# One ring of 18 buffers for the raw and split q and k tiles of a fused attention and MLP kernel

## The chip, the cores and the metric

The kernel runs on one core of a Trainium2 chip. The metric is the device time of one execution in microseconds (us); less is better. In the profile PE is the matrix engine (PEld its weight loads), DVE the vector engine, ACT the scalar engine, POOL the GpSimd engine, and SP the engine that does nothing here but issue transfers (SPq is its queue).

## The reference

For 4 batches, 8 heads, 576 positions and a head size of 64, attention with a learned position bias is computed; its output is read as 2304 tokens of 512 values and goes through two MLP layers with 2048 hidden units. Cut to what matters:

```python
scores = scale * np.matmul(q, k.transpose(0, 1, 3, 2))
psi_rel, psi_i = np.log1p(np.abs(rel)), np.log1p(np.maximum(pos[:, None], 1.0))
bias = np.maximum((psi_rel / psi_i)[..., None] @ w1 + b1, 0.0) @ w2
scores = scores + bias.transpose(2, 0, 1)[None]
attn = np.exp(scores - np.max(scores, axis=-1, keepdims=True))
x = np.matmul(attn / (np.sum(attn, axis=-1, keepdims=True) + 1e-09), v)
h = x @ w_in;   x = (h * np.cos(h)) @ w_out
h = x @ w_in2;  out = (np.maximum(h, 0.0) + alpha * np.minimum(h, 0.0)) @ w_out2
```

## The kernel before

The program has five stages: attention, then the hidden layer and the output layer of the first MLP (h_phase0, o_phase), then the same of the second. The change touches attention alone, so the rest is told only as far as attention runs into it.

Attention works on 16 pairs: a pair n is two heads hp of one batch b. Pair n brings a q tile and a k tile of 128 partitions by 640 values. Their matrix products are made from split operands: `load_qk` lets q and k land as raw tiles rq and rk (SP issues both transfers), and `split_qk` lets POOL make a rounded part (qh, kh, line 421, a cast) and the rest (ql, kl, line 426, a subtraction). `emit_S` makes a score tile S from three products (qh kh, qh kl, ql kh). Pair 0 alone is used unsplit (`NFP` is 1): its raw tiles feed the products.

Each pair has five score tiles: S1 and S2 belong to unit A, S0, S3 and S4 to unit B. The first four pairs run all their units A first and their units B later, so that four pairs' q and k are alive at once; from pair 4 on a pair runs A, then B. There is one PSUM buffer for S, so the next S waits until both halves of the one before have been read by DVE (`emit_max`, line 459: scores plus bias, and the row maximum nm, for the bias tiles bt of the two heads). ACT then makes the exponential P (line 472). Transposes of P (T), the product with v (x) and the normalisation (R, N) fill PE between score tiles.

The bias is made beside this, at the start of the program: 36 groups g in the order 0 to 15, 32 to 35, 16 to 31. For a group DVE makes the hidden units u (line 132, a few by ACT, line 130), PE makes the sums bps (line 137), ACT makes the rows be (line 151) and SP writes them to a DRAM table bias_d (line 156). There are six buffers for be. A bias tile bt is read back from the table by SP (lines 385 to 393) when the groups that it needs have landed: bt0_1 and bt0_5 need groups 0 to 7, bt0_2 and bt0_6 groups 8 to 15.

Towards the end of attention a background list stages the MLP's weights, one step at a time, through tiles with one or two buffers: raw weights land (raw, line 181), ACT, DVE and POOL convert them (wc, wp, lines 211 to 221), DVE combines them (wt, line 264), ACT and POOL split them (sw, lines 237 and 239) and SP writes the parts to DRAM (line 254). The tile for sw has one buffer, so a split begins when the transfer of the one before has landed.

The program's order on each engine is not that of the code. A scheduler sorts all instructions by priority and by its own planned times, and it hands a tile a free buffer of its pool at that moment, not in turn. An engine then runs its instructions strictly in that order; SP too, so a transfer that waits for its buffer holds back every transfer behind it.

q and k have two pools. The first has one buffer for rq and one for rk, so raw q of pair n+1 can only land when ql of pair n is made, and raw k when kl is made. The second has four buffers each for qh, ql, kh and kl; pair 0's raw tiles take one of the four of qh and of kh. That makes 18 buffers of 2560 bytes per partition.

Of the kernel before, what the change touches and what calls it, by code (L numbers as in the profile page):

```python
# [9 lines left out]
F32 = mybir.dt.float32  # L10
F32R = mybir.dt.float32r
# [24 lines left out]
QC = S + 64  # L36
# [4 lines left out]
FIRST, SIDE, SMOD, BFIRST, BRATE, SPL, WS0, WSR, PER = 4, 6, 2, 8, 2.5, 3, 28, 3.2, 1.0  # L41
# [1 line left out]
START = ((0, 1), (1, 1), (0, 2), (1, 2), (2, 1), (2, 2), (3, 1), (3, 2))  # L43
KEEP = (1, 1)
ELAG = 1
NFP = 1
NDIR = 6
XA, HX = 2, 300
RING, LO = 4, 3
# [19 lines left out]
def attn_mlp_kernel(ctx: ExitStack, tc: tile.TileContext, a: dict, out: bass.AP):  # L69
# [256 lines left out]
    def attention():  # L326
        with ExitStack() as c:
# [9 lines left out]
            pos = {(n, s): j for j, (n, u, s) in enumerate(stages)}  # L337

            bt_p = c.enter_context(tc.tile_pool(name="bt", bufs=BTB))
            rq_p = c.enter_context(tc.tile_pool(name="rq", bufs=1))  # L340
            qk_p = c.enter_context(tc.tile_pool(name="qk", bufs=FIRST))
            v_p = c.enter_context(tc.tile_pool(name="vp", bufs=FIRST + 1))
            m_p = c.enter_context(tc.tile_pool(name="mp", bufs=6))
            P_p = c.enter_context(tc.tile_pool(name="PP", bufs=PBUF))
# [6 lines left out]
            qk = {}  # L351
# [43 lines left out]

            def load_qk(n):
                hp, b = pairs[n]
                p, x = (rq_p, "r") if n >= NFP else (qk_p, "h")
                rq, rk = (p.tile([128, QC], F32, tag=(t + x) if n < NFP else (x + t), name=f"r{t}{n}") for t in "qk")
                sy.dma_start(out=rq, in_=a["q"][b, hp])  # L400
                sy.dma_start(out=rk, in_=a["k"][b, hp])
                raws[n] = (rq, rk)
# [7 lines left out]
            def load_qkv(n):  # L410
                load_qk(n)
                load_v(n)

            def split_qk(n):
                if n < NFP:
                    qk[n] = raws.pop(n)
                    return
                t = []
                for r, nm in zip(raws.pop(n), "qk"):
                    hi, lo = (qk_p.tile([128, QC], F32R, tag=nm + x, name=f"{nm}{x}{n}") for x in "hl")  # L420
                    ge.tensor_copy(out=hi, in_=r)
                    t.append((r, hi, lo))
                yield
                qk[n] = [x for r, hi, lo in t for x in (hi, lo)]
                for r, hi, lo in t:
                    ge.tensor_tensor(out=lo, in0=r, in1=hi.bitcast(F32), op=ALU.subtract)
                    yield

            def emit_S(n, s):
                q, k = qk[n][::len(qk[n]) // 2]  # L430
                terms = ((q, k),)
                if n >= NFP:
                    qh, ql, kh, kl = qk[n]
# [161 lines left out]
            for n in range(2):  # L595
                load_qk(n)
                for _ in split_qk(n):
                    pass
            sy.dma_start(out=alpha, in_=a["alpha"])

            def rest():
                for n in range(2, FIRST):
                    load_qk(n)
                    yield
                    load_v(n - 2)
                    yield from split_qk(n)
                    done.add(n)
                for n in range(FIRST - 2, FIRST):
                    load_v(n)
                    yield  # L610
# [38 lines left out]
            while i < NS or pend_exp or waiting or fill:  # L649
                new = []  # L650
                if i < NS:
                    n, u, s = stages[i]
                    hp, b = pairs[n]
                    more_bias(max(BFIRST + int(BRATE * j), GNEED[s]))
                    for m in range(FIRST, NP):
                        f = pos[m, 1]
                        if i == f - 6:
                            load_qkv(m)
                            splits[m] = split_qk(m)
                        if f - SPL <= i < f:  # L660
                            next(splits[m], None)
                    while n not in done:
                        next(side, None)
                    pss = emit_S(n, s)
                    new = [(n, s, h) + emit_max(n, s, h, ps) for h, ps in enumerate(pss)]
# [334 lines left out]
    def h_phase1():  # L1000
        runs = [[(0, 512), (512, 1024)], [(1024, 1536), (1536, 2048)], [(2048, 2304)]]
        with ExitStack() as c:
# [78 lines left out]
            step(1000)  # L1081

    attention()
    pinned.append(1)
    h_phase0()
# [71 lines left out]
```

## Time and profile before

| what | value |
|---|---|
| median of three runs | 1146.52 us (1136.35 to 1147.46) |
| the profiled execution | 1133.93 us, span 1131.8 us from first to last instruction |
| busy PE, DVE, ACT, POOL | 1082.6, 820.8, 641.8, 247.6 us |
| attention, by PE's order | about 0 to 362 us, with the first products of h_phase0 from 347 us |

The span is 2.1 us shorter than the profiled execution's time. PE is busy for 96% of the span, so what can be gained is mostly in the 49 us in which PE is idle, and in the stretches in which its clock was granted at half. Times in the rows below count from the start of the span.

### The profile page before, as it was taken

To read this page: it belongs to the slowest core of one execution; us is meant where nothing else is said; L and a number is where in the kernel's file an instruction comes from. 1 tells how busy PE (TensorE), PEld (TensorE's weight loads), DVE (VectorE), ACT (ScalarE), POOL (GpSimd) and SP (SyncE) were. 2 spreads that over 40 slices of the span, in tenths; PEclk is the share of its full clock that TensorE was granted. 3 is DMA by queue.
4 is the path that set the end of the run, shared out by engine and by line. 5 is a ranking of instruction groups with operands and counts; after the bars stand their busy time and mean duration, and the time that the engine had idled before them with its cause. 6 is when DMAs were issued, how large, how long until landed. Compare 5 with 4: busy or idle time off the path is not lost.

```text
span 1131.8 us, 18836 instructions
## 1 busy us (share of the span) xinstructions
PE 1082.6 (96%) x7054; PEld 895.4 (79%) x7054; DVE 820.8 (73%) x1336; ACT 641.8 (57%) x1072; POOL 247.6 (22%) x248
## 2 busy tenths in 40 slices
PE   7698999999998998999999999899999999999998
PEld 2245666667666877888799999888888888999998
DVE  8886677777775799787876767767766756776673
ACT  6886667777775555555454444655655534444442
POOL 4304656656433121000000000112323210000000
PEclk9889999999999999999999999999999999999999
DMA  8656645666447774533766344555666549664621
GB/s 276 213 170 183 195 143 190 204 187 230 151 150 266 299 251 149 168 131 126 259 209 197 120 141 139 196 197 197 216 219 214 199 152 342 204 211 126 209 60 53
DMA packets 104971, 213.48 MB, mean 189 GB/s; under 512 B 11440, under 2 KB 55472, under 8 KB 103472
## 3 DMA queue, kind: packets, MB, share of 16 engines
q1 hardware_dynamic: 77104, 157.74, 43.9%
q10 hardware_dynamic: 25856, 47.19, 11.1%
q0 software_dynamic: 1920, 7.34, 1.7%
q8 instruction: 56, 0.92, 0.3%
q14 instruction: 35, 0.29, 0.1%
HBM read 130.83 MB, written 81.41 MB: 188 GB/s over the span
## 4 chain that ended last, share of the span: by engine, by line
PE 70%; DVE 13%; DMA 9%; ACT 4%; issue 3%; POOL 1%; SPq 0%; ACTq 0%; DVEq 0%; POOLq 0%
PE v L1053 17%; PE ob L947 13%; PE h L752 8%; PE oa L947 7%; PE oc L947 7%; PE S L443 5%; DVE u L132 3%; PE x_B L560 3%; PE x_A L560 2%; PE T_B L525 2%; DMA w_d<-sw 2%; PE T_A L525 2%; DMA raw<-in_wo_dram 2%; DMA b<-g_d 1%; DVE tb L762 1%
## 5 line engine op out<-in xcount | busy, mean ns | idle before, releaser
L1053 PE MATMUL v<-x,v 128*128 128x512 f32 (+1 forms) x960 | 197.6, 368 | 0.0
L752 PE MATMUL h<-xhi,w 128*128 128x512 f32 (+1 forms) x640 | 184.7, 372 | 7.6 <-DVE tb L765 7.3
L1053 PEld LDWEIGHTS v<-x,v 128*128 128x128 f32 x960 | 167.3, 189 | 30.3
L752 PEld LDWEIGHTS h<-xhi,w 128*128 128x128 f32 x640 | 116.1, 188 | 31.2 <-issue 7.9
L221 POOL TENSOR_TENSOR wc<-wc,wp 128x512 int32<-128x512 int32 x64 | 83.4, 1304 | 242.4 <-DVE wc L218 186.8
L472 ACT ACTIVATE P<-P,nm 128x576 f32<-128x576 f32 x128 | 98.5, 771 | 42.7 <-DVE nm L459 42.3
L929 ACT ACTIVATE op<-a 128x768 fp32r<-128x768 f32 x84 | 70.5, 844 | 86.5 <-PE ob L947 27.5
L752 PE MATMUL h<-xlo,w 128*128 128x512 f32 (+1 forms) x320 | 118.5, 370 | 0.0
L459 DVE CUSTOM_DVE_ANT_0 P<-S,bt 128x576 f32<-128x576 f32 x128 | 91.9, 753 | 33.0 <-PE S L443 24.6
L930 DVE TENSOR_TENSOR op<-a,op 128x768 fp32r<-128x768 f32 x84 | 79.4, 955 | 46.0 <-ACT op L929 44.2
L929 ACT ACTIVATE op<-b 128x768 fp32r<-128x768 f32 x84 | 70.7, 844 | 67.9 <-PE ob L947 22.2
L930 DVE TENSOR_TENSOR op<-b,op 128x768 fp32r<-128x768 f32 x84 | 79.6, 958 | 31.2 <-ACT op L929 31.1
L947 PE MATMUL ob<-op,wo 128*128 128x384 f32 x432 | 77.3, 337 | 1.6 <-DVE op L930 1.6
L947 PEld LDWEIGHTS ob<-op,wo 128*128 128x128 f32 x432 | 75.3, 188 | 2.2 <-DVE op L930 2.2
L1064 DVE SCALAR_TENSOR_TENSOR u<-v,asg,u 128x1024 f32<-128x1024 f32 (+1 forms) x48 | 48.0, 1013 | 35.3 <-ACT u L1063 35.3
L760 ACT ACTIVATE ta<-h,quart 128x1024 int32<-128x1024 f32 (+1 forms) x40 | 41.1, 1026 | 53.9 <-DVE tb L762 27.5
L752 PEld LDWEIGHTS h<-xlo,w 128*128 128x128 f32 x320 | 60.3, 189 | 10.9
L443 PE MATMUL S<-kh,qh 64*128 64x288 f32 (+1 forms) x270 | 53.5, 351 | 13.2 <-DVE nm L459 13.1
L1063 ACT ACTIVATE u<-v,sgn 128x1024 f32<-128x1024 f32 (+1 forms) x48 | 42.9, 897 | 40.1 <-PE v L1053 37.5
L761 DVE SCALAR_TENSOR_TENSOR tb<-ta,h 128x1024 f32<-128x1024 int32 (+1 forms) x40 | 44.4, 1110 | 22.4 <-ACT ta L760 21.6
L132 DVE TENSOR_SCALAR u<-at,thr 128x576 f32<-128x576 f32 (+17 forms) x120 | 54.3, 522 | 2.2 <-PE bps L137 2.2
L212 ACT ACTIVATE wp<-raw 128x512 int32<-128x512 uint32 x64 | 42.6, 665 | 22.8 <-POOL wc L221 12.1
(143 smaller groups left out, 2160.2 us busy)
## 6 DMA issues: line engine op xcount, KB each, us to landing
a<-g_d SPq DMA_DIRECT2D x60, 384.0 KB, 4.6
b<-g_d SPq DMA_DIRECT2D x48, 384.0 KB, 4.8
raw<-in_wi_dram SPq DMA_DIRECT2D x32, 512.0 KB, 3.9
raw<-in_wo_dram SPq DMA_DIRECT2D x32, 512.0 KB, 4.2
g_d<-tb ACTq DMA_DIRECT2D x32, 512.0 KB, 3.0
g_d<-u ACTq DMA_DIRECT2D x32, 512.0 KB, 3.4
bias_d<-be SPq DMA_DIRECT2D x36, 295.5 KB, 3.4
w_d<-sw SPq DMA_DIRECT2D x35, 256.0 KB, 2.4
```

What stands on the lines that cost most here:

```text
L132: ve.tensor_scalar(u[:, 0:n], at[:, 0:n], thr[:, m:m + 1], None, op0=ALU.max)
L221: ge.tensor_tensor(out=c, in0=c, in1=p, op=ALU.add)
L443: te.matmul(ps[:, hf, 0:HS], lhsT=w[r, 128 * i:128 * i + 128], rhs=m[r, c0:c0 + HS], start=(j == 0), stop=(j == len(terms) - 1))
L459: keep(2, ve.tensor_tensor_reduce(out=sn.rearrange("p (a b) -> p a b", a=2), in0=ps[:, :, 0:HS], in1=bt[hp, s].rearrange("p (a b) -> p a b ...
L472: keep(3, se.activation(out=e, in_=e, func=AF.Exp, bias=nm, scale=-1.0, accum_out=sums[n, u][:, col, 0:1]))
L560: te.matmul(ps[64 * h:64 * h + 64, 0:w], lhsT=v[:, 256 * h + 64 * cc:256 * h + 64 * cc + 64], rhs=Tt[n, u][:, cc, h, 0:w], start=(cc == 0) ...
L752: te.matmul(ps, lhsT=w_[:, wx, w], rhs=xx[:, 0:n], start=(j == 0), stop=(j == 11))
L929: se.activation(out=o[:, 0], in_=x, func=AF.Copy)
L930: ve.tensor_tensor(out=o[:, 1], in0=x, in1=o[:, 0].bitcast(F32), op=ALU.subtract)
L947: ins = te.matmul(ps[:, m], lhsT=x[:, sl] if L else w[:, sl], rhs=w if L else x, start=first, stop=kk == NK - 1 and n == 2, skip_group_che ...
L1053: ins = te.matmul(both[:, i, 0:a1 - a0], lhsT=w[:, wx, 128 * cc:128 * cc + 128], rhs=x[:, xx, cc, a0 - o:a1 - o], start=(n == 0), stop=(n ...
L1064: ve.scalar_tensor_tensor(out=g, in0=ps, scalar=asg[:, f:f + 1], in1=g, op0=ALU.mult, op1=ALU.max)
```

## The change

The two pools become one, with a single tag and 18 buffers. All raw and split tiles of q and k, pair 0's too, take any free buffer of it. The number of buffers, their size and the place of the pool in memory are the same, and so are all instructions; what differs is which buffer a tile gets, what it therefore waits for, and the order that the scheduler makes.

```diff
-NFP = 1
+NFP, QKB = 1, 18
...
-            rq_p = c.enter_context(tc.tile_pool(name="rq", bufs=1))
-            qk_p = c.enter_context(tc.tile_pool(name="qk", bufs=FIRST))
+            qk_p = c.enter_context(tc.tile_pool(name="qk", bufs=QKB))
...
-                p, x = (rq_p, "r") if n >= NFP else (qk_p, "h")
-                rq, rk = (p.tile([128, QC], F32, tag=(t + x) if n < NFP else (x + t), name=f"r{t}{n}") for t in "qk")
+                rq, rk = (qk_p.tile([128, QC], F32, tag="qk", name=f"r{t}{n}") for t in "qk")
...
-                    hi, lo = (qk_p.tile([128, QC], F32R, tag=nm + x, name=f"{nm}{x}{n}") for x in "hl")
+                    hi, lo = (qk_p.tile([128, QC], F32R, tag="qk", name=f"{nm}{x}{n}") for x in "hl")
```

The buffers that the built program gives: before, every raw q from pair 1 on lands in one buffer and every raw k in another. After, raw q and k of pairs 1, 2 and 3 have buffers of their own, which nothing has used; raw q and k of pair 4 take those of pair 2; and from pair 5 on raw q again always takes the buffer of the raw q before it (raw k with one exception, at pair 7). The lines of the changed kernel are one or two lower than those of the kernel before from line 341 on.

The first place is SP's queue from bias group 10 on, at 31 to 46 us in the trace of before. In a row, the name left of the arrow is the tile written; be10 is the bias rows of group 10, rq4 and rk4 are raw q and k of pair 4, and the brackets name the semaphores that are waited for (Pool_49 is POOL's). Before:

```order
L156 DMA bias_d_57<-be10_408 16x8x591 [waits Activation_49]
L156 DMA bias_d_57<-be11_425 16x8x591 [waits DMAHW7_49,Activation_49]
L400 DMA rq4_1387<-in_q_dram 128x640 [waits Pool_49]
L156 DMA bias_d_57<-be12_443 16x8x591 [waits DMAHW1_49,Activation_49]
L156 DMA bias_d_57<-be13_480 16x8x591 [waits DMAHW2_49,Activation_49]
L401 DMA rk4_1388<-in_k_dram 128x640 [waits DMAHW3_49,Pool_49]
L156 DMA bias_d_57<-be14_501 16x8x591 [waits DMAHW4_49,Activation_49]
L156 DMA bias_d_57<-be15_518 16x8x591 [waits DMAHW5_49,Activation_49]
```

After:

```order
L156 DMA bias_d_57<-be10_405 16x8x591 [waits Activation_49]
L398 DMA rq4_1384<-in_q_dram 128x640 [waits Pool_49]
L156 DMA bias_d_57<-be11_422 16x8x591 [waits Activation_49]
L399 DMA rk4_1385<-in_k_dram 128x640 [waits DMAHW1_49,Pool_49]
L156 DMA bias_d_57<-be12_440 16x8x591 [waits DMAHW2_49,Activation_49]
L156 DMA bias_d_57<-be13_477 16x8x591 [waits DMAHW3_49,Activation_49]
L156 DMA bias_d_57<-be14_498 16x8x591 [waits DMAHW4_49,Activation_49]
L156 DMA bias_d_57<-be15_515 16x8x591 [waits DMAHW5_49,Activation_49]
```

Both raw loads of pair 4 moved up, and POOL's instruction that they wait for is another: before, ql and kl of pair 3; after, ql and kl of pair 2, whose raw buffers they take.

The second place is DVE at the first score tile of pair 0, S0_1, at 32 to 40 us. u32_1 is hidden unit 1 of group 32, nm0_1 and nm0_5 are the maxima of the tile's two heads; the rows named ISA are those of line 459. Before:

```order
L132 TENSOR_SCALAR u32_0_537<-at_160,thr_157 128x528
L132 TENSOR_SCALAR u32_1_539<-at_160,thr_157 128x528
L132 TENSOR_SCALAR u32_2_541<-at_160,thr_157 128x528
L132 TENSOR_SCALAR u33_0_560<-at_160,thr_157 128x544
L459 ISA P0_0_354,nm0_1_355<-S0_1_349,bt0_1_344 128x576
L459 ISA nm0_1_355 128x1
L132 TENSOR_SCALAR u33_1_562<-at_160,thr_157 128x544
L132 TENSOR_SCALAR u33_2_564<-at_160,thr_157 128x544
L132 TENSOR_SCALAR u33_3_566<-at_160,thr_157 128x544
L459 ISA P0_0_354,nm0_5_357<-S0_1_349,bt0_5_346 128x576
```

After:

```order
L132 TENSOR_SCALAR u32_0_534<-at_157,thr_154 128x528
L457 ISA P0_0_351,nm0_1_352<-S0_1_346,bt0_1_341 128x576
L457 ISA nm0_1_352 128x1
L132 TENSOR_SCALAR u32_1_536<-at_157,thr_154 128x528
L132 TENSOR_SCALAR u32_2_538<-at_157,thr_154 128x528
L132 TENSOR_SCALAR u33_0_557<-at_157,thr_154 128x544
L457 ISA P0_0_351,nm0_5_354<-S0_1_346,bt0_5_343 128x576
```

Both maxima moved ahead by three hidden units. On ACT the exponential of the second half (P0_0 with nm0_5) stood behind be15 before and stands ahead of it after.

The third place is ACT at the end of attention, at 346 to 361 us. P15_3 is the last score tile's exponential, T15_B the copies of its transposes, R15_B the copy of its normalisation; sw0_5_3 is split 3 of step 5 of the weights staged for the first MLP's output layer, wp0_15_1 a conversion of that layer's raw weights 15. Before:

```order
L472 ACTIVATE P15_3_4599,sume2_118<-P15_3_4599,nm15_8_4602 128x576
L237 ACTIVATE sw0_5_3_3926<-wc0_11_1_3735 128x2x256
L211 ACTIVATE wc0_13_1_4021<-raw0_13_1_3982 128x512
L510 ACTIVATE T15_B_4772<-T15_B_1_4779 128x2x256
L237 ACTIVATE sw0_6_0_4077<-wc0_12_1_3975 128x256
L510 ACTIVATE R15_B_4820<-N15_B_4805 128x320
L212 ACTIVATE wp0_14_1_4269<-raw0_14_1_3700 128x512
L510 ACTIVATE T15_B_4772<-T15_B_3_4808 128x2x256
```

After:

```order
L470 ACTIVATE P15_3_4596,sume2_115<-P15_3_4596,nm15_8_4599 128x576
L237 ACTIVATE sw0_6_0_4074<-wc0_12_1_3972 128x256
L212 ACTIVATE wp0_14_1_4266<-raw0_14_1_3697 128x512
L211 ACTIVATE wc0_14_1_4265<-raw0_14_1_3697 128x512
L508 ACTIVATE T15_B_4769<-T15_B_1_4776 128x2x256
L508 ACTIVATE T15_B_4769<-Tr15_4782 128x8x64
L212 ACTIVATE wp0_15_1_4314<-raw0_15_1_4272 128x512
L237 ACTIVATE sw0_6_1_4112<-wt0_6_4025 128x2x256
L508 ACTIVATE R15_B_4817<-N15_B_4802 128x320
L508 ACTIVATE T15_B_4769<-T15_B_3_4805 128x2x256
```

The staging of weights stands about one and a half steps further on beside the same piece of attention, and one conversion or split more stands ahead of each of the two T15_B copies on which the last products wait. The scheduler moved it so all along attention, from the second raw weight on; on SP the loads of the first layer's weights wo now stand behind the transfer of sw0_5_3, where they stood ahead of it.

## Rows read from the trace of the kernel before

**Rows 1.** Busy us (instructions) by engine in stretches, then PEclk, DMA share, GB/s.
```profile
0.00:50.00 50.00, 36.00 (x268) 12.37 (x268) 42.02 (x94) 35.23 (x73) 24.50 (x24) 0.93 0.80 260
50.00:100.00 50.00, 42.47 (x317) 22.35 (x317) 38.51 (x105) 40.27 (x88) 8.28 (x11) 0.87 0.63 181
...
100.00:285.00 185.00, 183.45 (x1519) 127.19 (x1518) 136.27 (x343) 130.12 (x297) 108.77 (x113) 1.00 0.59 186
285.00:347.00 62.00, 56.85 (x472) 39.14 (x469) 47.55 (x121) 45.75 (x103) 25.79 (x26) 1.00 0.47 155
347.00:365.00 18.00, 14.34 (x81) 10.22 (x81) 8.99 (x19) 8.38 (x16) 5.80 (x6) 1.00 0.84 291
```

**Rows 2.** What SP waited for in the whole trace: us, times, longest.
```profile
SPq L400 <- POOL ql L426: 11.2, 6, 4.3
```

**Rows 3.** What PE waited for, 0 to 100 us, and 340 to 365 us.
```profile
PE S L443 <- DVE nm L459: 8.1, 3, 4.9
...
PE x_B L560 <- ACT T_B L510: 3.3, 2, 2.2
```

**Rows 4.** SP's issues in order: start, us, what.
```profile
31.73 1.18 SPq L156 DMA_DIRECT2D bias_d<-be  x2
37.18 0.33 SPq L400 DMA_DIRECT2D rq<-in_q_dram  x1
...
39.51 3.55 SPq L156 DMA_DIRECT2D bias_d<-be  x3
45.29 0.33 SPq L393 DMA_DIRECT2D bt<-bias_d  x1
```

**Rows 5.** POOL in order: splits of pair 2 (first row) and pair 3.
```profile
20.52 1.70 POOL L426 TENSOR_TENSOR kl<-rk,kh 128x640 fp32r<-128x640 f32 x1
25.14 9.65 POOL L421 CAST qh<-rq 128x640 fp32r<-128x640 f32 x1 [2.92 <-DMA rq<-in_q_dram]
...
35.43 1.72 POOL L426 TENSOR_TENSOR ql<-rq,qh 128x640 fp32r<-128x640 f32 x1
37.11 1.73 POOL L426 TENSOR_TENSOR kl<-rk,kh 128x640 fp32r<-128x640 f32 x1
```

**Rows 6.** DVE in order, around the maxima of S0_1.
```profile
32.91 1.31 DVE L132 TENSOR_SCALAR u<-at,thr 128x528 f32<-128x528 f32 x3
34.13 0.75 DVE L459 CUSTOM_DVE_ANT_0 P<-S,bt 128x576 f32<-128x576 f32 x1
...
34.81 4.33 DVE L132 TENSOR_SCALAR u<-at,thr 128x544 f32<-128x544 f32 x3
39.06 0.74 DVE L459 CUSTOM_DVE_ANT_0 P<-S,bt 128x576 f32<-128x576 f32 x1
```

**Rows 7.** ACT in order: be15, and the second half of P0_0.
```profile
36.61 1.15 ACT L151 ACTIVATE be<-bps,b,consts 128x336 f32<-128x336 f32 x2
39.85 0.78 ACT L472 ACTIVATE P<-P,nm 128x576 f32<-128x576 f32 x1 [2.08 <-DVE nm L459]
```

**Rows 8.** The chain that ended last, in order of time: start, us, what.
```profile
40.12 5.01 DMA bias_d<-be
...
348.23 5.67 DMA w_d<-sw
```

**Rows 9.** The page's DMA issues: KB each, median us from issue to landing.
```profile
raw<-in_wo_dram SPq DMA_DIRECT2D x32, 512.0 KB, 4.2
...
bias_d<-be SPq DMA_DIRECT2D x36, 295.5 KB, 3.4
w_d<-sw SPq DMA_DIRECT2D x35, 256.0 KB, 2.4
```

**Rows 10.** A stretch of half clock, columns as in rows 1.
```profile
39.00:45.80 6.80, 5.84 (x36) 2.98 (x36) 5.11 (x14) 5.09 (x12) 0.00 (x0) 0.50 0.88 295
```

**Rows 11.** SP in order, at the end of attention.
```profile
358.39 0.33 SPq L181 DMA_DIRECT2D raw<-in_wo_dram  x1
```

**Rows 12.** ACT in order, at the end of attention: a conversion wp.
```profile
359.78 0.67 ACT L212 ACTIVATE wp<-raw 128x512 int32<-128x512 uint32 x1 [0.22 <-POOL wc L221]
```

## The prediction, made blind

> **What bounds the kernel now.** I read the page first. PE is busy for 1082.6 of 1131.8 us, so I looked for the time in which PE is idle or slow. Busy time by stretches [rows 1] puts most of the idle time of attention at the start: in the first 100 us PE is busy for 36.0 + 42.5 = 78.5 us, so 21.5 us are idle, and the granted clock is 0.93 and 0.87 of the full 2.4 GHz. From 100 to 285 us PE is idle for 1.55 us only, at full clock. From 285 to 347 us 5.15 us are idle, from 347 to 365 us 3.66 us. The order of the instructions is the same again within h_phase0, so what the change does must show before some 365 us.
>
> Then I asked what holds the buffers that change. SP waits for ql 6 times, 11.2 us in all, once for 4.3 us [rows 2]. The reader should see the place of that longest wait in SP's issues [rows 4]: after the two bias writes at 31.73 (1.18 us) SP issues nothing until raw q of pair 4 at 37.18. That instant is the end of ql3 on POOL, 35.43 + 1.72 = 37.15 [rows 5]. It comes so late since the cast qh3 took 9.65 us. POOL is not the bound there; the question is who waits behind SP. Behind rq4 stand be12, be13, rk4, be14 and be15, then the loads of bt0_2 and bt0_6. Three bias writes go out from 39.51, the last at about 40.1, and bt0_2 is requested at 45.29. What lies between is the landing of be15, 5.01 us from 40.12 on, and it is a link of the chain that ended last [rows 8]. On the other side PE waits three times for the maxima before it may write S, 8.1 us in the first 100 us, one of them 4.9 us [rows 3]: the maxima want the bias tile. So this is the one place where a buffer of q or k can reach the end of the program.
>
> **The change, part by part.** Nothing is added or removed: the number of matrix products, splits, transfers and bytes stays. All terms are moves.
>
> *Loads of the start.* Raw q and k of pairs 2 and 3 need no buffer of another tile now and go out without a wait. rq4 and rk4 wait for ql2 and kl2; kl2 ends at 20.52 + 1.70 = 22.22 us [rows 5], ten microseconds before SP comes to rq4. The pause of SP from 32.91 to 37.18, 4.27 us, should go. That is not yet a gain: be12 to be15 can't be written before ACT has made them, and be15 must land before bt0_2. Before, be15 was ready at 36.61 + 2 x 0.575 = 37.76 us (two be in 1.15 us [rows 7], be15 the second) and waited on SP until 40.1. After, the scheduler puts the second exponential of P0_0 ahead of be15 on ACT. That exponential wants the second maximum nm0_5, which stood at 39.06 + 0.74 = 39.80 on DVE [rows 6] and had ACT wait 2.08 us [rows 7]. Both maxima now stand three hidden units earlier, 3 x 0.44 = 1.3 us by the row of three in 1.31 us [rows 6], so nm0_5 comes at 38.5, the exponential ends at 38.5 + 0.78 = 39.3, and be15 (about 0.6 us alone, 1.15 if it runs beside slow neighbours; I take the latter) is ready at 40.4. So be15's issue gains nothing: the wait for POOL on SP is replaced by a wait for DVE on ACT. What I do count is the landing. Before, be12 to be15, rq4 and rk4 went out within 3 us, and be15 took 5.01 us against a median of 3.4 [rows 8, 9]. After, all but be15 go earlier and apart, so I take the median: 3.4 - 5.01 + (40.4 - 40.1) = -1.3, rounded to **-1.2 us** for bt0_2 and the chain behind it. Its bounds: 0 if the landing stays 5 us, and -3.9 if be15 is not held up at all (issued at 37.8 instead of 40.1, and 1.6 less landing).
>
> *Clock of that stretch.* From 39.0 to 45.8 us the granted clock is 0.50, that is 1.2 GHz, with PE busy for 5.84 us [rows 10], behind a stretch in which PE was often idle. At 2.4 GHz the same work would take half, 2.9 us less. I count **0**, since PE's idle time ahead of the stretch stays; -2.9 is the bound.
>
> *Splits on POOL.* Of pair 4 the casts qh4 and kh4 now stand at some 40 us instead of some 90 us. A cast or subtraction on POOL takes 1.7 us when not held up [rows 5], and meanwhile DVE is held: the three u beside the subtractions took 4.33 us instead of 1.31 [rows 6], that is 3 us for two POOL instructions of 3.45 us. For a cast I take 0.5 us each by the first row of three, which overlaps the end of qh3 with little harm; two casts cost DVE 0.9 us in the new place and spare as much in the old. Net **0**, from -0.9 to +0.9.
>
> *Pairs 5 and on.* Raw q again takes the buffer of the raw q before it, so the same wait for ql remains; of the 11.2 us in rows 2 the 6.9 us beside the longest stay or shift, and PE's 1.55 us of idle time [rows 1] says that nobody on PE minds. **0**, bounds -1.5 and +1.5.
>
> *The end of attention.* Weight staging runs one and a half steps earlier along attention. Before, the last products waited for the copies T15_B on ACT, 3.3 us in all and 2.2 us once [rows 3], since a split ahead of the copy waited for the buffer of sw, whose transfer took 5.67 us [rows 8] against a median of 2.4 [rows 9]: it lay behind loads of wo on the queue. After, these loads stand behind the transfer, so I take the wait of 2.21 us as gone. One more conversion (0.67 us [rows 12]) and one more split (0.63 us, an estimate from that row, since both read tiles of 512 values a row) now stand ahead of the two copies: 2.21 - 0.67 - 0.63 = 0.9, so **-0.9 us**; at best -3.3, at worst the price of the rival below.
>
> The sum is -1.2 + 0 + 0 + 0 - 0.9 = -2.1 us. The profiled execution took 1133.93 us and would take 1131.8. The median of the three runs lies 12.6 us above that execution; I see nothing in the change that acts on this gap, and put the sum on the median: 1146.5 - 2.1 = 1144.4, told as **1144.5 us**.
>
> **The rivals.** *Nothing moves (B).* The bias is bound by DVE's hidden units, not by SP, and POOL's splits of pair 3 take their time from DVE wherever they stand. Since rq3 lands earlier, POOL comes to its subtractions earlier, and each stretches a hidden unit ahead of be15 rather than behind it. For it speaks the 4.33 us [rows 6]; against it that qh3 ended at 25.14 + 9.65 = 34.79, just as DVE ran its first instruction that is not a u (34.13 to 34.88 [rows 5, 6]), so the cast may stay stuck as before whenever it begins. The landing's -1.2 is then taken by up to 1.2 us more of DVE work ahead of be15, and the tail comes out even: 1146.5.
>
> The rows show a cast of POOL that was stuck for some 8 us while DVE ran one u of 0.44 us after another. The Trainium skill ("SBUF — State Buffer", "Who interferes with whom") says that the port pair that DVE and GpSimd share is an exclusive lock: who starts first holds it for a whole instruction and the other blocks. By that rule alone the cast should have come in after one u, some 0.5 us, and the sum would then be B's, nothing, as DVE would pay for POOL at once. The trace agrees that one blocks the other, but not that the wait ends with one instruction.
>
> *Slower (C): the last pair waits for the staging.* After, the copy T15_B_3 on ACT stands behind wp0_15_1, which needs the raw weight 15 to land, and behind sw0_6_1, which needs the transfer of sw0_6_0. Before, that raw weight was requested at 358.39 [rows 11], a landing takes 4.2 us in the median [rows 9], and PE wanted the copies from about 357 us on. If SP requests it one and a half steps earlier it is there; if the request stays less than 4.2 us ahead of the last maxima, ACT sits in front of wp0_15_1 with T15_B_3 behind it. PE then waits for up to 4.2 us, and 1.3 us of conversion and split come on top: 5.5 us, or 2.2 if all 3.3 us of waits in rows 3 go in exchange. I take 5, near the upper end, since those waits stood at another copy; the start gives nothing, so 1151.5. It decides when the conversion that frees the raw buffer ends late. For it speaks that a split in ACT's queue already held these copies; against it that the staging stands earlier, not later.
>
> *A larger gain (D).* be15 is not held up (-3.9), the clock does not fall in that stretch (-2.9) and the tail loses all its waits (-3.3, where the conversions hide in them). With one or two of the three it is 6 to 7, with all 10 us: about -8, 1138.5. Against it stands the new place of be15 on ACT. The Trainium skill ("Trainium Kernel Development and Optimization", "Best Practices") has a rule to double-buffer so that transfers overlap with compute; by it one would expect all 11.2 us of SP's waits back, 1135. The built program speaks against that, as it gives the buffers singly from pair 5 on.
>
> *It doesn't do what it says.* In steady state that is so: raw q goes round in one buffer as before. My forecast contains this.
>
> **How the numbers follow.** The forecast has 0.50 (1144.5; by itself 1141.5 to 1147.5, from the bounds of the start, -3.9, and of the small terms), B 0.17 (1146.5), C 0.20 (1151.5) and D 0.13 (1138.5). A measurement of this kernel can't tell less than about 1%, 11.5 us, from no change: the three runs alone span 11.1 us. So nearly all cases lie within it. The range reaches over C to 1152, and down past D to 1131, since the runs before went down to 1136 and the profiled execution took 1134, and a median of the changed kernel may fall on that side. Faster by over 1%: D with all its terms on the low side of the scatter, 0.12; slower by over 1%: C with a second wait of its kind, 0.08; within 1%: 0.80.
>
> **What would show it.** SP's issues: rq4 behind be10 without the pause of 4.3 us, be15 still at about 40, bt0_2 requested at 44 or earlier. DVE: nm0_5 at about 38.5. ACT: the wait ahead of the second P0_0 shrinks, be15 right behind it. PE: the longest wait for S below 4.9 us by about 1.2; half clock at about 39 us still there; idle time from 100 to 285 us still under 3 us. Tail: no transfer w_d of over 4 us in the chain, and waits of x_B for T15_B of about 2 us. I am wrong if be15 goes out before 39 us or after 42, if the clock at 39 to 46 us comes out at 1.00, or if PE waits over 4 us for T15_B.

## The result, and the profile after

The changed kernel takes 1144.9 us in the median of 20 runs, the kernel before 1138.4 us in 20 runs of its own: a ratio of 1.0055, with an interval of 1.0037 to 1.0073. It is some 6 us slower. Two of the three runs of before that the prediction had seen (1146.52 and 1147.46 us) are the two longest of those 20, so that its 1144.5 us lies next to the measured time by luck: it forecast a gain of 2 us, and there is a loss of 6.

The profiled execution, the fastest of the 20, spans 1135.9 us, 4.1 more than before, with 1082.2 us of PE busy (1082.6 before). The windows of [rows 1], after the change:

```profile
0.00:50.00 50.00, 35.43 (x268) 12.61 (x268) 43.63 (x98) 35.55 (x73) 27.23 (x26) 0.93 0.81 260
50.00:100.00 50.00, 41.68 (x326) 21.31 (x327) 39.06 (x104) 40.94 (x88) 7.38 (x10) 0.93 0.63 178
100.00:285.00 185.00, 177.87 (x1477) 123.28 (x1475) 136.67 (x340) 127.58 (x291) 111.10 (x115) 1.00 0.60 192
285.00:347.00 62.00, 53.91 (x443) 37.41 (x443) 44.83 (x113) 45.55 (x102) 23.08 (x24) 0.97 0.47 142
347.00:365.00 18.00, 18.00 (x128) 12.65 (x126) 11.20 (x26) 9.72 (x21) 5.27 (x5) 1.00 0.80 277
```

The number behind the comma is PE's busy time. From 100 to 285 us PE is now idle for 7.1 us (1.55 before), from 285 to 347 us for 8.1 (5.15 before), and from 347 to 365 us not at all (3.66 before). The granted clock from 285 to 347 us is 0.97 (1.00 before), which at 62 x 0.03 costs some 2 us more, an estimate. The loss was made in the steady part of attention, and some of it came back at its end: the last exponential starts 2.3 us later than before (353.15 and 350.85 us).

**The start** went in the order that the prediction worked out, but with less gain. SP's queue, as in [rows 4]:

```profile
31.64 1.18 SPq L156 DMA_DIRECT2D bias_d<-be  x2
32.87 0.59 SPq L398 DMA_DIRECT2D rq<-in_q_dram  x1
33.50 1.42 SPq L156 DMA_DIRECT2D bias_d<-be  x1
35.02 0.54 SPq L399 DMA_DIRECT2D rk<-in_k_dram  x1
35.65 8.95 SPq L156 DMA_DIRECT2D bias_d<-be  x5
44.82 0.41 SPq L392 DMA_DIRECT2D bt<-bias_d  x1
```

The pause of 4.3 us is gone. On ACT, as in [rows 7], the exponential waits for DVE and be15 stands behind it:

```profile
38.83 0.78 ACT L470 ACTIVATE P<-P,nm 128x576 f32<-128x576 f32 x1 [1.82 <-DVE nm L457]
39.51 0.19 ACT L470 ACTIVATION_READ_ACCUMULATOR P<-P,nm 128x1 f32 x1
39.61 1.07 ACT L151 ACTIVATE be<-bps,b,consts 128x336 f32<-128x336 f32 x2
```

So be15 is ready at 40.7 us (40.4 was forecast) and goes out at once. Its landing takes 3.0 us (5.01 before, 3.4 was forecast), by the view of bias_d from 40.0 to 40.9 us:

```profile
L156 SPq DMA_DIRECT2D bias_d<-be x1: 517/517/517, 40.7 to 40.7; - x1
DMA to landing us min/median/max: 3.0/3.0/3.0
```

Yet bt0_2 is requested at 44.82 in place of 45.29, which is 0.5 us and not 1.2. On SP the bias write of the next group stands ahead of it, and waits for ACT until 44.1. SP's longest wait from 38 to 46 us:

```profile
SPq L156 <- ACT u L130: 3.2, 1, 3.2
```

**The steady part.** PE's waits for the maxima from 100 us to the end of attention (us, times, longest), first of the kernel before:

```profile
PE S L443 <- DVE nm L459: 5.0, 7, 1.3
```

and after the change:

```profile
PE S L441 <- DVE nm L457: 10.3, 7, 3.5
```

Four of the new waits, read on the engine that is late. DVE ahead of the maxima of S5_1, and of S15_1:

```profile
150.34 0.58 DVE L217 TENSOR_SCALAR wc<-wc 128x512 int32<-128x512 int32 x1 [0.49 <-ACT wc L211]
150.96 1.93 DVE L218 SCALAR_TENSOR_TENSOR wc<-raw,wc 128x512 int32<-128x512 int32 x1
...
153.10 0.72 DVE L457 CUSTOM_DVE_ANT_0 P<-S,bt 128x576 f32<-128x576 f32 x1
...
333.17 0.43 DVE L264 TENSOR_TENSOR wt<-wc,wc 128x256 f32<-128x256 f32 x1 [0.98 <-POOL wc L221]
333.63 0.43 DVE L264 TENSOR_TENSOR wt<-wt,wc 128x256 f32<-128x256 f32 x1
334.09 0.42 DVE L264 TENSOR_TENSOR wt<-wc,wt 128x256 f32<-128x256 f32 x1
...
335.23 0.75 DVE L457 CUSTOM_DVE_ANT_0 P<-S,bt 128x576 f32<-128x576 f32 x1
...
335.91 1.59 DVE L218 SCALAR_TENSOR_TENSOR wc<-raw,wc 128x512 int32<-128x512 int32 x1
337.42 0.74 DVE L457 CUSTOM_DVE_ANT_0 P<-S,bt 128x576 f32<-128x576 f32 x1
```

Steps of the weight staging (L217, L218, L264) stand ahead of the maxima, and at 335.91 between the two maxima of one tile. The 1.93 us at 150.96 is a step that takes 0.69 us alone; beside it POOL ran a subtraction of pair 8. PE waited 1.2 us for the first pair of maxima and 3.5 us for the second. The second longest wait of the seven, 2.9 us at S14_1, has the same form, and there the step ahead of the maxima waits for ACT in its turn:

```profile
314.91 1.08 DVE L217 TENSOR_SCALAR wc<-wc 128x512 int32<-128x512 int32 x1 [1.66 <-ACT wc L211]
315.92 0.74 DVE L457 CUSTOM_DVE_ANT_0 P<-S,bt 128x576 f32<-128x576 f32 x1
```

The fourth place is on ACT, at S11_4 and S12_1:

```profile
276.01 0.69 ACT L212 ACTIVATE wp<-raw 128x512 int32<-128x512 uint32 x1 [2.21 <-POOL st L304]
276.60 0.76 ACT L470 ACTIVATE P<-P,nm 128x576 f32<-128x576 f32 x1
...
277.49 0.17 DVE L478 TENSOR_REDUCE sm_B<-sume 128x5 f32<-128x10 f32 x1 [3.85 <-ACT P L470]
```

A conversion wp waits for POOL, the last exponential of pair 11 stands behind it, DVE waits 3.85 us for that exponential's sum, and the maxima of pair 12 stand behind that. PE waited 1.4 us for them.

**The end of attention.** ACT after the change, where [rows 12] had a conversion:

```profile
361.45 0.66 ACT L212 ACTIVATE wp<-raw 128x512 int32<-128x512 uint32 x1 [1.75 <-DMA raw<-in_wo_dram]
364.33 0.63 ACT L237 ACTIVATE sw<-wt 128x512 fp32r<-128x512 f32 x1 [2.22 <-DMA w_d<-sw]
364.87 0.42 ACT L508 ACTIVATE R_B<-N_B 128x320 f32<-128x320 f32 x1
365.19 0.59 ACT L508 ACTIVATE T_B<-T_B 128x512 f32<-128x512 f32 x1
```

The copy T15_B_3 stands behind a landing raw weight and a transfer, as rival C had it. But PE's wait of x_B for T_B is 0.5 us there (3.3 before, [rows 3]): products of h_phase0 fill the time.

### The profile page after: what moved, and what is told of

It reads as the page before. It is cut to its first block, busy times and chain, and to the rows that moved or that the text cites. A ratio compares the mean times of both kernels' runs of the same rounds, so it can differ in the third digit from the quotient of the medians.

```text
span 1135.9 us, 18827 instructions
## 1 busy us (share of the span) xinstructions
PE 1082.2 (95%) x7054; PEld 895.1 (79%) x7054; DVE 822.5 (72%) x1336; ACT 642.4 (57%) x1072; POOL 248.9 (22%) x248
## 4 chain that ended last, share of the span: by engine, by line
PE 58%; DVE 4%; DMA 3%; issue 1%; ACT 1%; SPq 0%; ACTq 0%; DVEq 0%
PE v L1051 17%; PE h L750 16%; PE ob L945 12%; PE oc L945 7%; PE oa L945 7%; DMA b<-g_d 2%; DVE op L928 1%; DVE b L885 1%; DMA a<-g_d 1%; DMA x_d<-o 0%; DVE a L885 0%; DVE tb L763 0%; SPq L181 0%; ACT op L927 0%; DVE tb L759 0%
## 5 line engine op out<-in xcount | busy, mean ns | idle before, releaser
L1062 DVE SCALAR_TENSOR_TENSOR u<-v,asg,u 128x1024 f32<-128x1024 f32 (+1 forms) x48 | 48.0, 1014 | 36.4 <-ACT u L1061 36.3
L441 PEld LDWEIGHTS S<-kh,qh 64*128 64x128 f32 (+1 forms) x270 | 29.1, 188 | 36.5 <-issue 23.1
```

What stands on the lines that cost most here:

```text
L441: te.matmul(ps[:, hf, 0:HS], lhsT=w[r, 128 * i:128 * i + 128], rhs=m[r, c0:c0 + HS], start=(j == 0), stop=(j == len(terms) - 1))
L1062: ve.scalar_tensor_tensor(out=g, in0=ps, scalar=asg[:, f:f + 1], in1=g, op0=ALU.mult, op1=ALU.max)
```

## The experiments

Each was timed beside the kernel before on the same chip. "Idle" is 185 us less PE's busy time from 100 to 285 us in the profile.

| run | q and k in | order of the work from pair 4 on | ratio to before (interval) | idle, us |
|---|---|---|---|---|
| before | two pools | old | 1 | 1.55 |
| the change | ring | its own | 1.0055 (1.0037 to 1.0073) | 7.1 |
| e1_ring_later | ring | staging later | 1.0047 (1.0023 to 1.0071) | 7.3 |
| e4_ring_between | ring | staging a little later | 1.0033 (1.0010 to 1.0055) | 5.6 |
| e2_old_earlier | two pools | staging earlier | 1.0058 (1.0032 to 1.0083) | 5.9 |
| e3_old_earlier2 | two pools | staging earlier still | 1.0044 (1.0022 to 1.0067) | 7.7 |
| e6_old_ring_order | two pools | the change's | 1.0072 (1.0049 to 1.0094) | 8.7 |
| e9_old_start_new_rest | ring | the change's | 1.0039 (1.0019 to 1.0060) | 8.9 |
| e5_ring_old_order | ring | old | 0.9975 (0.9952 to 0.9999) | 1.7 |
| e12_ring_old_order_again | ring | old | 0.9992 (0.9967 to 1.0018) | 1.6 |
| e10_new_start_old_rest | ring | old | 0.9994 (0.9974 to 1.0014) | 1.6 |
| e11_old_fixed | two pools | old | 1.0025 (1.0003 to 1.0047) | 1.5 |
| e7_ring_dve_behind | ring | the change's, steps moved on DVE | 1.0270 (1.0232 to 1.0309) | 11.2 |
| e8_ring_both_behind | ring | the change's, steps moved on DVE and ACT | 1.0216 (1.0180 to 1.0251) | 9.8 |

**Staging later or earlier.** The staging of weights had moved one to one and a half steps along attention. One number sets when it begins, 28 in both kernels: 34 and 30 with the ring (e1, e4), 26 and 22 with the two pools (e2, e3).

```diff
-FIRST, SIDE, SMOD, BFIRST, BRATE, SPL, WS0, WSR, PER = 4, 6, 2, 8, 2.5, 3, 28, 3.2, 1.0
+FIRST, SIDE, SMOD, BFIRST, BRATE, SPL, WS0, WSR, PER = 4, 6, 2, 8, 2.5, 3, 34, 3.2, 1.0
```

> The ring of 18 as in the change, with the weight staging of attention begun later (WS0 34 in place of 28), so that from the fifth weight on it stands within a step of its place in the kernel before. Theory P (the loss of 6 us is the staging's new place against the score tiles, not the buffers): the loss goes, a ratio to the kernel before of 0.997 to 1.003, PE's waits for the maxima after 100 us about 5 us instead of 10.3. Theory B (the buffers of q and k, or the splits on POOL that they let start earlier, cost it): the ratio stays at 1.004 to 1.007 and these waits at 9 us or more.

> The ring of 18 with the staging begun a little later (WS0 30): its place lies between those of the kernel before and of the changed one. Theory P: a time between or beside the two, 1.000 to 1.006, and its difference from the changed kernel shows in PE's waits for the maxima. Theory B: 1.004 to 1.007, as the changed kernel.

> The two old pools as in the kernel before, with the staging begun earlier (WS0 26), which puts it about one weight earlier along attention, near its place in the changed kernel. Theory P: slower than before by 0.3 to 0.7%, with PE's waits for the maxima after 100 us at 8 us or more. Theory B: the same as before within 0.2%, waits near 5 us.

> The two old pools, staging begun with WS0 22: from the third weight on nearly one weight earlier than before, but at other places between the score tiles than with WS0 26. Theory P: not equal to before, slower by 0.2 to 0.7%. Theory B: the same as before within 0.2%. If this one is level and WS0 26 is slower, the exact place counts and not how early it is.

The two with the old pools are slower by 0.4 to 0.6%, as theory P had it and theory B did not: no ring is needed for the loss. PE's waits for the maxima came to 7.2 us in e2, where P had 8 or more. The time of e4 fits P as well. But e1 failed P: with the staging within a step of its old place the loss stays, and 9.5 us of waits for the maxima with it. How early the staging runs does not decide it alone; all four new arrangements lose 0.3 to 0.6%.

**The order fixed.** To part buffers from order, each instruction was tied, without a wait, behind the one that a table puts ahead of it on its engine. The scheduler then only hands out the buffers.

```diff
         attn_mlp_kernel(tc, args, outs[0])
+        pin_order(nc, tc)
...
+            if prev is not None:
+                tc.add_manual_dep(real[k], prev.name, mybir.DependencyInfo(
+                    mybir.DependencyClass.NoSync, mybir.DependencyReason.DATA), reason="order")
+            prev = real[k]
```

e5 and e12 are the changed kernel with the table of the kernel before, e11 (a control) is the kernel before with its own, e6 the kernel before with the changed kernel's table from pair 4's loads on.

> The ring of 18 buffers with every engine's order fixed to that of the kernel before, instruction for instruction: the buffers are the only difference. Theory P2 (the order alone costs the 6 us, the buffers nothing): ratio to the kernel before 0.997 to 1.002, PE idle from 100 to 285 us below 3 us. Theory B (the buffers of q and k cost it): 1.004 to 1.007 with 5 us or more idle there.

> The two old pools with the order of the changed kernel fixed for everything that is emitted from pair 4's loads on; the start is left to the scheduler, since the old pools can't run the changed start. Theory P2: slower than before by 0.4 to 0.7%, PE idle from 100 to 285 us at 6 to 8 us, as in the changed kernel. Theory B: 0.998 to 1.002, idle below 3 us.

> The two old pools with every engine's order fixed to that which they have anyway: a control for the fixing itself. Expected equal to before, 0.997 to 1.003; if it is faster by 0.2% or more, the gain of the ring in the old order belongs to the fixing and not to the buffers.

> The ring in the old order once more, beside the control on the same chip. If the buffers alone gain, by the waits at the start that go, it is 0.995 to 0.999 of before, and 2 to 5 us below the control; if the first result was chance, 0.999 to 1.003.

The windows from 100 to 285 us, of the ring in the old order (e5):

```profile
100.00:285.00 185.00, 183.33 (x1520) 126.09 (x1518) 137.09 (x346) 130.16 (x299) 110.12 (x114) 1.00 0.59 187
```

and of the old pools in the new order (e6):

```profile
100.00:285.00 185.00, 176.27 (x1451) 121.36 (x1449) 134.69 (x334) 127.58 (x292) 110.21 (x113) 0.99 0.60 189
```

The loss goes with the order and not with the buffers: theory P2 holds, from both sides, with e6 a little over its bounds (1.0072, and 8.7 us idle where 6 to 8 were expected). The control came out 0.25% above before, though its order is the same on every engine; so less than about 0.3% says nothing in this table, and what the ring gains by itself (0.25 and 0.08% below before, 0.3% below the control) stays open between 0 and 3 us: e12 lies 3.2 us below the control, as a gain of the buffers would have it, but at 0.9992 of before, as chance would.

**Start or rest.** With the ring, the two tables mixed: what is emitted ahead of pair 4's loads from one kernel, the rest from the other.

```diff
-    every engine: one list, from one kernel
+    every engine: a list of what is emitted ahead of pair 4's loads, and a list of the rest
```

> The ring; what is emitted before pair 4's loads (bias, units A and B of pairs 0 to 3 as far as emitted there) in the order of the kernel before, everything later in the order of the changed kernel, the two lists mixed by the scheduler. Theory R (the order of the rest, staging and pairs 4 to 15, costs some 9 us): 1.003 to 1.008, 5 us or more of PE idle from 100 to 285 us. Theory S (the changed order of the start costs it): 0.996 to 1.001.

> The ring; the start in the changed kernel's order, everything that is emitted from pair 4's loads on in the order of the kernel before. Theory R: 0.995 to 1.001, PE idle from 100 to 285 us below 3 us. Theory S: 1.003 to 1.008.

Theory R holds: the new order of the rest costs 0.4% with the old start, against before and against e10, and the new start costs nothing with the old rest. Against the control (1.0025) the time of e9 alone would not tell; its 8.9 us of idle time, against 1.5, do. The start of one exponential (the second head of the first score tile of pairs 4 and 12, and of the second tile of pair 15; us in the profile) shows where the time goes:

| run | pair 4 | pair 12 | pair 15 |
|---|---|---|---|
| before | 136.31 | 275.23 | 335.79 |
| e11 | 135.29 | 274.24 | 335.01 |
| e5 | 132.24 | 271.31 | 334.78 |
| e12 | 132.77 | 271.72 | 334.85 |
| e10 | 134.50 | 273.49 | 334.30 |
| the change | 137.73 | 279.80 | 343.25 |
| e9 | 136.03 | 280.51 | 345.06 |
| e6 | 137.97 | 281.56 | 345.76 |

All kernels with the old order take 138.9 to 139.1 us from pair 4 to pair 12, whatever their buffers; those with the new one take 142.1 to 144.5.

**Staging moved behind the maxima.** If the steps that stand ahead of the maxima cost the time, they may be put behind them. In the changed kernel's table 53 steps were moved on DVE (e7), and 49 on ACT behind the exponentials as well (e8), each by a few places.

```diff
     DVE, at S15_1:
-    wc0_12_1 (L217), maximum, wc0_12_1 (L218), maximum
+    maximum, maximum, wc0_12_1 (L217), wc0_12_1 (L218)
```

> The ring with the changed kernel's order fixed on every engine, but on DVE 53 steps of the weight staging that stood close ahead of a score tile's maxima are put behind them; nothing else moves. If those steps are what PE waits for (theory P3), PE's waits for the maxima after 100 us fall from 10.3 us to 7 or less and the ratio to 1.001 to 1.004. If the maxima are late for another reason (an exponential on ACT, the sums, POOL), waits stay at 9 us or more and the ratio at 1.005.

> As the one before, and on ACT 49 steps of the staging that stood close ahead of an exponential are put behind it as well. Theory P3: the waits for the maxima fall further, to 5 us or less, ratio 0.997 to 1.003. If the staging's place near the maxima doesn't matter, or what is won at the maxima is lost at the copies T and the products x, the ratio stays at 1.004 to 1.007 and other waits of PE (x, T) grow by what these fall.

e7 took 1.027 (1.0232 to 1.0309) of before, e8 1.0216 (1.0180 to 1.0251). PE's waits for the maxima fell as theory P3 had it, to 5.6 us, and yet the kernel lost 30 us, where P3 had 1.001 to 1.004 for e7 and no theory had more than 1.007 for e8. The waits of PE and ACT in e7, from 100 to 390 us:

```profile
PE S L441 <- DVE nm L457: 5.6, 6, 1.7
PE T_B L523 <- ACT P L470: 5.1, 3, 2.8
PE T_B L523 <- ACT T_B L508: 4.1, 3, 2.2
PE T_B L488 <- ACT T_B L508: 4.1, 3, 3.7
...
ACT wp L212 <- POOL wc L221: 16.5, 10, 4.7
```

In the changed kernel the last of these is 2.5 us. One of the ten, in the timelines of DVE, POOL and ACT:

```profile
226.84 0.69 DVE L218 SCALAR_TENSOR_TENSOR wc<-raw,wc 128x512 int32<-128x512 int32 x1
...
227.70 1.26 POOL L221 TENSOR_TENSOR wc<-wc,wp 128x512 int32<-128x512 int32 x1 [7.04 <-DVE wc L218]
...
228.99 0.68 ACT L212 ACTIVATE wp<-raw 128x512 int32<-128x512 uint32 x1 [4.65 <-POOL wc L221]
229.56 0.77 ACT L470 ACTIVATE P<-P,nm 128x576 f32<-128x576 f32 x1
```

DVE's step comes after the maxima now, POOL's addition after that step, ACT's next conversion after the addition, since wp has one buffer, and the exponential and the copies T after the conversion. The wait has gone round by two engines and come back to PE, larger. These waits are the smaller part of the 30 us. The same 290 us in the changed kernel and in e7:

```profile
100.00:390.00 290.00, 274.31 (x2146) 192.63 (x2144) 206.90 (x490) 193.99 (x424) 143.99 (x146) 0.99 0.61 200
100.00:390.00 290.00, 262.26 (x2017) 180.61 (x2017) 190.80 (x478) 181.75 (x411) 138.93 (x144) 0.93 0.52 164
```

PE is idle for 12 us more in e7, and the granted clock is 0.93 in place of 0.99, which at 290 x 0.06 is some 17 us at full clock, an estimate; the profile of e7 is 29.6 us longer. From 229.0 to 239.2 us, for example, the clock was granted at half, behind 7 us in which PE was idle for 1.7. In e8 ACT's wait for the addition is 5.9 us, and PE waits for the copies T_B instead, 7.6 us in its transposes and 6.1 us in its products.

## Why the prediction was wrong

**The step that failed** is "Pairs 5 and on", put at 0 with bounds of -1.5 and +1.5. It asked only which buffers q and k get there and who waits for ql. It left out that the staging of weights and the attention work around it stand in another order from pair 4 on, which the prediction knew and priced at the end of attention alone. By the exponentials the changed kernel loses 8.1 us from the end of pair 7 (202.28, before 202.92) to pair 15. The reason given, that PE was idle for 1.55 us only, is no bound for a loss. It says that the old order fits closely, and so that another one has much to lose: the profile of before should have been read as a warning there.

**The start** was right in its mechanism: the wait for POOL on SP is replaced by ACT's wait for DVE, and be15 gains nothing. The landing's gain was put at 1.2 us (its own sum gives 1.3) and was 0.5 at the request for bt0_2: the landing itself got shorter than forecast, but the term left out the bias write of the next group, which waits for ACT and stands on SP ahead of bt0_2. The longest wait for S in the first 100 us is 4.9 us as before, where 3.7 was forecast, and all of them went from 8.1 to 9.8 us; the exponential of pair 4 came 1.4 us later than before. The casts were priced at 1.7 us by rows of subtractions; qh4 takes 0.72 us after the change (at 38.05), and nothing hangs on it. With the old start and the old rest (e5), be15 does go out early, the term that rival D had: bt0_2 is requested at 43.4 us, and pair 4 comes 3.5 to 4.1 us earlier than before in e5 and e12, 2.5 to 3.0 earlier than in the control. Of that, 2.5 to 2.9 us are lost again before pair 15: in both runs the granted clock fell to half for 3.4 us at 311 to 315 us, at the score tiles of pair 14, which it did at no time from 280 to 380 us in the kernel before, in e10 or in the control. At half clock those 3.4 us cost some 1.7, an estimate; the rest is not placed. So these two profiled executions show a gain at the start, and most of it given back later; two executions of one order, the kernel before and the control, lie 1.0 us apart at pair 4. **The clock** fell to half as forecast, but 2.7 us earlier, from 36.3 to 43.1 us; over the predicted 39.0 to 45.8 us it is 0.70.

**The end of attention** was put at -0.9 and is -2.8 us of PE's waits for T_B: the right sign, too small. Rival C named the right copy, the right raw weight and the right transfer, and ACT did wait for both (1.75 and 2.22 us); its price of +5 us failed, because PE had h_phase0's products to do. The loss of the kernel comes from the steady part.

**The rivals** B and D told of the start, its clock and the tail, C of the tail, and none of the order in the steady part. The forecast's chances of within 1% (0.80) and the range held the time; the sign was wrong, since 0 for the largest unknown was taken without its bound from the trace. Of the signs that it named, idle time from 100 to 285 us under 3 us failed outright, with 7.1. It held 1% to be the least that can be told, from three runs; 20 runs of each told 0.55%.

**What stays open.** Which of the moved steps make the loss is not shown. The four places above are read from the trace; moving such steps by hand (e7, e8) made other waits, so no single step can be named. Nor is it shown why every other arrangement tried leaves 5.6 us of idle time or more where the old one leaves 1.6. The ring in the old order has the lowest ratios here, and can't be told from the kernel before.

## What to carry to other kernels

Where a scheduler sets the order, a change of buffers is two changes, and in a part where the bound engine is idle for 1% the second one may cost more than the first can bring. Fix the order, try the buffers alone, and then try the order alone, before either is judged. Steps that are links of a chain over DVE, POOL and ACT, moved here on DVE alone, cost 2.7%: what waits for them has to be moved with them. And when PE gets idle time, its granted clock belongs in the sum beside the waits.

## What the runs showed of the hardware that was not expected

A DVE step with two inputs (L218), 0.69 us alone, took 1.93 us beside a POOL subtraction that had begun before it and 1.59 us beside another:

```profile
150.60 1.74 POOL L424 TENSOR_TENSOR ql<-rq,qh 128x640 fp32r<-128x640 f32 x1
...
335.68 1.27 POOL L239 TENSOR_TENSOR sw<-wt,sw 128x512 fp32r<-128x512 f32 x1
```

It ended 0.55 us after POOL's instruction in both places, as if it had stood still until POOL was done. The Trainium skill ("SBUF — State Buffer", "Who interferes with whom") has it so for a DVE instruction with two SBUF inputs against a GpSimd instruction that reads SBUF, and these two rows agree.

The granted clock fell to half behind PE's wait at pair 14 in e5 and e12, at one place in both. The kernel before, e10 and the control ran through the same order of instructions 2 to 4 us later, with the same wait of 1.28 to 1.29 us, and stayed at full clock; why is open. The window of e5, then of e12:

```profile
311.30:314.70 3.40, 3.40 (x16) 1.77 (x17) 3.27 (x10) 1.91 (x5) 2.05 (x2) 0.50 0.39 118
311.80:315.20 3.40, 3.40 (x17) 1.86 (x16) 3.27 (x10) 1.78 (x5) 2.06 (x2) 0.50 0.53 125
```

PE is busy for all of these 3.4 us, so that this loss does not show in PE's idle time.
